# A planned two-stage attention and MoE kernel: the planner's transfer rate, the first w_in pair ahead of k, and new urgencies

## The chip, the cores and the metric

One core of a Trainium2 chip runs the whole kernel. The metric is device time in microseconds (us) of one execution, given as the median of several runs. Engines are named PE (TensorE, matrix products), DVE (VectorE), ACT (ScalarE), POOL (GpSimd) and SP (SyncE, which here only issues DMAs).

## The reference

For 8 batches and 8 heads (576 positions, head size 64), 32 pack queries p attend to k and v, and the packed result then serves as keys and values for the queries q:

```python
def sm_attn(qq, kk, vv):
    s = scale * np.matmul(qq, kk.transpose(0, 1, 3, 2))
    s = s - np.max(s, axis=-1, keepdims=True)
    a = np.exp(s)
    a = a / (np.sum(a, axis=-1, keepdims=True) + 1e-09)
    return np.matmul(a, vv)
p_packed = sm_attn(p, k, v)
out = sm_attn(q, p_packed, p_packed)
...
h = x @ w_in                                   # x: (4608, 512), the heads side by side
sp = np.maximum(h, 0.0) + np.log1p(np.exp(-np.abs(h)))
g = h * erf(sp)
return (g @ w_out).astype(np.float32)          # w_in: (512, 2048), w_out: (2048, 512)
```

The weights w_in and w_out arrive as 64-bit floats, all else as 32-bit floats.

## The kernel before, in words

The second attention is never multiplied out. For each batch b, the packed values are multiplied into w_in once (`w_prime`, tiles `wph`, `wpl`), and the second softmax's weights (tiles `a2h`, `a2l`) then multiply that product to give h. Every operand of the large products is split into a high and a low part (`h` and `l` in the names), and three of the four products of parts are added, so each large product costs three matmuls.

Work comes in units (b, f), 128 columns of the inner dimension of 2048 each: `h_unit` makes h for one unit (two halves c of 288 positions, six matmuls each), copies it to `hs` (line 618), `gate_group` applies softplus (L582) and erf (L587) to a group of units, because each function needs a table load on ACT, and DVE multiplies and splits (L592 to L596); `o_unit` then adds the unit into the output accumulators. The remaining 64 positions per batch are sent to a scratch tensor `rest` and multiplied two batches at a time (`o_rest`). Batches 0 and 1 are interleaved in halves of 8 units, batches 2 to 7 follow with 16 units each.

The head is `attention(0, ...)`. It loads p, k, v and q, makes the scores `s` on PE, the row maxima `ms` and `m` on DVE, the exps on ACT (L451), turns the result over on PE (`t` to `a1t`, `a1r`), multiplies with v (`p`), scales it (`pk`) and turns it into `pt`. Then come the second scores `s<-q,pt`, and on DVE and ACT the second softmax: transposes (L520), maximum (L532), subtraction (L533), exp (L535), sum (L536), reciprocal and scaling (L539), transposes back to `tb` (L542), and the parts `a2h` (L543, ACT) and `a2l` (L544, DVE). In batch 0 this is done in two halves of the positions. The first h product needs the first half of a2 and `w_prime(0, 0)`.

A 64-bit weight tile becomes a 32-bit one in four instructions (`convert`): a scaled copy on ACT (L296), then three bit operations on DVE (L297, L298, L300). The first block of 512 columns of w_in comes in two pairs of row blocks of 1 MB each (`load_w_in_pair`, L329), the later blocks, pieces 1 to 3, in four tiles of 0.5 MB each (`load_w_in`, L314, tiles `wi`), w_out in 16 tiles of 0.5 MB (`load_w_out`, tiles `wos`, then `woh` and `wol`).

The order is not written by hand. Each operation is added to a `Program` with a key (lower is more urgent) and a duration; `Program.order` simulates the engines greedily, always taking the lowest key that is ready, and the start times that it finds fix each engine's order for good: at run time every engine takes its instructions in that order, and each waits for its inputs. The keys are counted in units of h: unit n has key n, its o products n + "lag", h copies n - "copy", softplus n + lag - act - 2, the gate's DVE work n + lag - dve. The keys of attention come from the lists "steady", "second" (batch 1) and "third" (batch 2). Batch 0 has the keys -40, -39, ... by step. The DMA model is two lines:

```python
state["bus"] = max(state["bus"], now + busy + self.SEND[0]) + op.dur / self.SEND[1]
end = state["bus"] + self.SEND[2] + PLAN["late"]
```

with 0.45 us as busy for an issue by SP or ACT, and op.dur the bytes of the transfer. Before the first h, idle times of PE in the plan are filled with small matmuls on `warm`.

Of the kernel before, what the change touches and what calls it, by code (L numbers as in the profile page):

```python
# [18 lines left out]
F64_SCALE = 2.0 ** -112  # L19

PLAN = {
    "lag": 6.48,
    "act": 3.24,
    "dve": 2.85,
    "copy": 11.87,
    "steady": (-0.3, 0.83, 2.16, -1.73, -0.29, 5.48, 1.14, 5.66, 5.08, 10.47, 11.68, 9.06, 11.68, 12.76),
    "second": (-13.65, -15.48, -10.46, -9.6, 0.34, -0.29, -16.5, -2.04, -5.02, 1.53, 1.53, 2.92, 1.21, 6.31),
    "third": (8.44, 9.98, 10.57, 17.02, 19.97, 18.41, 20.11, 22.11, 18.02, 21.6, 23.41, 29.53, 26.07, 28.85),
    "wp": 1.22,
    "wi": 13.75,  # L30
    "wo": 8.18,
    "conv": 2.44,
    "rest": -5.38,
    "ends": (2, 4, 5, 8, 12, 15, 16, 20),
    "merge": (1, 1),
    "turns": (0, 8, 16),
    "second half": 3.65,
    "wp first": 8.52,
    "late": 1.0,
    "first w": (0.1, 0.2),  # L40
    "also": {'norm': 4.02, 'w_out': 5.13, 'packs': 3.76, 'gate': 2.09, 'turned': 2.44},
    "warm": (1.4, 7.0, 1.0),
    "pad": (1.04, 0.1, 0.1),
    "first conv": (-3.79, 0.42),
}


# [22 lines left out]
class Program:  # L70

    LOAD = 1.283
    SWITCH = (0.09, 0.22)
    SEND = (1.0, 380e3, 0.4)

    def __init__(self, room):
        self.ops, self.room = [], room
# [27 lines left out]
    def order(self):  # L105
# [26 lines left out]
        while events:  # L132
# [15 lines left out]
            for engine, line in ready.items():  # L148
# [39 lines left out]
                if engine in ("SP", "POOL") or op.kind == "dma":  # L188
                    state["bus"] = max(state["bus"], now + busy + self.SEND[0]) + op.dur / self.SEND[1]
                    end = state["bus"] + self.SEND[2] + PLAN["late"]  # L190
                else:
# [23 lines left out]
def tile_pack_attention_moe(ctx: ExitStack, tc: tile.TileContext, qT, kT, v, pT, w_in, w_out, out, rest):  # L215
    nc = tc.nc
    P = 128
    B, _, NC, S = qT.shape
# [29 lines left out]
    def buf(tag, shape, name, dtype=F32):  # L248
        pool, bufs = TAGS[tag]
        return Buf(tag, name, lambda: pools[pool].tile(shape, dtype, name=name, tag=tag, bufs=bufs))  # L250
# [7 lines left out]
    def line(engine, ins):  # L258
        names = {last[x] for x in (engine, *fresh) if x in last}
        for name in names:  # L260
            tc.add_manual_dep(ins.ins, name, mybir.DependencyInfo(
                mybir.DependencyClass.NoSync, mybir.DependencyReason.DATA), reason="order")
        for x in (engine, *fresh):
            last[x] = ins.ins.name
        fresh.clear()
        return ins
# [7 lines left out]
    def dve(key, n, emit, w, r, twice=False, after=()):  # L274
        return prog.add("DVE", key, dve_us(n, twice) * PLAN["pad"][0], 0.14 + PLAN["pad"][1], lambda: line("DVE", emit()), w, r, after=after)
# [5 lines left out]
    def dma(key, size, emit, w, r, engine="SP", after=()):  # L281
        return prog.add(engine, key, 0.45 if engine != "POOL" else 1.0, size, lambda: line(engine, emit()), w, r,
                        kind="dma" if engine == "ACT" else 0, after=after)
# [64 lines left out]
    a2, pt, wp = {}, {}, {}  # L348
# [27 lines left out]
    def attention(b, keys):  # L376

        first, roomy = b == 0, b < 2
# [3 lines left out]
        def load(name, src, tag, key, engines=("SP",)):  # L382
            made = []
            for c in range(NC):
                if tag == "wo":
                    made.append([buf("wo", [P, DM], f"{name}{c}{x}_{b}") for x in "ab"])
                    for x in range(2):
                        dma(key, P * HT * 4, lambda c=c, x=x: nc.sync.dma_start(
                            made[c][x][:, 0:HT], src[b, :, c, x * HT:(x + 1) * HT]), (made[c][x],), ())
                else:  # L390
                    made.append(buf(tag, [P, S], f"{name}{c}_{b}"))
                    if not first or name == "q":
                        dma(key, P * S * 4, lambda c=c: nc.sync.dma_start(made[c][:], src[b, :, c, :]), (made[c],), ())
            if first and name == "k":
                for x in range(2):
                    for c in range(NC):
                        at = slice(x * HT, (x + 1) * HT)
                        e, q = (("SP", nc.sync), ("ACT", nc.scalar))[c % 2]
                        dma(key, P * HT * 4, lambda c=c, at=at, q=q: q.dma_start(made[c][:, at], src[b, :, c, at]),
                            ((made[c], x),), (), e)  # L400
            return made
# [4 lines left out]
        def cut(made, c, x):  # L406
            return made[c][x][:, 0:HT] if isinstance(made[c], list) else made[c][:, x * HT:(x + 1) * HT]

        k = load("k", kT, "wo" if b == 1 else "kvq", keys[0])
        vt = "wo" if b < 2 else "kvq"  # L410
        values = [buf(vt, [P, DM if vt == "wo" else S], f"v{j}_{b}") for j in range(NCH)]
# [4 lines left out]
        if first:  # L416
            for i in range(2):
                load_w_in_pair(keys[1] + PLAN["first w"][i], -40 + 8 + PLAN["first conv"][i], 2 * i)
        q = load("q", qT, "kvq" if b else "t0", keys[2])
        big = lambda name, shape: buf("big", shape, f"{name}{b}")  # L420
        a = big("a1_", [P, 2, S])
# [8 lines left out]
        for x in range(2):  # L430
            banks, w, whole = scores[x]
# [85 lines left out]
        for x in range(2):  # L517
            banks, w, whole = places[x]
# [3 lines left out]
        for part in ((0,), (1,)) if first else ((0, 1),):  # L522
# [19 lines left out]
            turned = dve(ks[2], n, lambda span=span: nc.vector.transpose(span(tb), span(ta)), sp, rd)  # L542
# [139 lines left out]
    ends = {*PLAN["ends"], *range(PLAN["ends"][-1], N - G + 1, G), N - 2, N - 1, N}  # L682
# [27 lines left out]
    made = 1  # L710
# [71 lines left out]
```

## Time and profile before

| | |
|---|---|
| median of 3 runs | 726.67 us (725.94 to 727.18) |
| profiled execution | 724.65 us, span 722.9 us |
| PE busy | 705.6 us, 98% |
| ACT busy | 522.1 us, 72% |
| DVE busy | 414.5 us, 57% |
| DMA | 74.79 MB, mean 103 GB/s |

Busy shares are over the whole span, and a busy PE includes the warm matmuls before the first h product. In rows of the timeline the first number is the start in us, the second the time that the row covers; the text in brackets is the idle time of that engine before the row and what ended it. Rows of a stretch give busy time by engine, then the granted clock of TensorE, the busy share of the DMA engines and what they moved. Rows of waits give the total in us, how many, and the longest.

### The profile page before, as it was taken

What the parts mean: (1) busy time and instruction counts of PE and PEld (TensorE: products, weight loads), DVE (VectorE), ACT (ScalarE), POOL (GpSimd) and SP (SyncE); (2) the same over time, 40 slices, a digit from 0 to 9 for tenths busy, and PEclk for the clock granted to TensorE, in tenths of its full rate; (3) what the DMA queues carried; (4) which work ended last, traced back from release to release, by engine and by line L of the source; (5) the groups of instructions that cost most, each with busy time, mean ns of one, the idle gap of its engine ahead of it and who ended that gap; (6) DMA issues with size and microseconds to landing.
All of it is one profiled execution on the core that took longest, in us unless ns stands there. A gap on an engine that the chain in (4) does not pass through costs nothing.

```text
span 722.9 us, 13198 instructions
## 1 busy us (share of the span) xinstructions
PE 705.6 (98%) x5126; PEld 575.8 (80%) x5126; DVE 414.5 (57%) x672; ACT 522.1 (72%) x869; POOL 8.1 (1%) x14
## 2 busy tenths in 40 slices
PE   6979999999999999999999999999999999999997
PEld 5557887878788888887888878787888878788885
DVE  2899987799652375544753166546754247353520
ACT  3399998989885488774976568775987448677841
POOL 0000000001001000000000000000000000000000
PEclk9799999999999999999999999999999999999999
DMA  8952456663507302053204132043122310021113
GB/s 301 335 192 70 129 167 213 223 209 87 115 16 188 102 14 74 16 180 102 72 16 152 58 95 68 16 155 106 39 72 60 121 30 14 17 73 44 44 44 106
DMA packets 66974, 74.79 MB, mean 103 GB/s; under 512 B 40288, under 2 KB 43360, under 8 KB 66912
## 3 DMA queue, kind: packets, MB, share of 16 engines
q1 hardware_dynamic: 65104, 71.14, 32.2%
q0 software_dynamic: 1152, 2.10, 2.1%
q8 instruction: 40, 0.66, 0.4%
q10 hardware_dynamic: 656, 0.72, 0.3%
q14 instruction: 22, 0.18, 0.1%
HBM read 54.00 MB, written 19.92 MB: 102 GB/s over the span
## 4 chain that ended last, share of the span: by engine, by line
PE 86%; ACT 6%; DMA 5%; SPq 1%; issue 0%; DVE 0%; ACTq 0%
PE o L291 47%; PE h L291 26%; PE or L291 6%; PE wp L291 4%; DMA wi<-w_in 2%; PE s L291 2%; DMA q<-qT 1%; PE p L291 1%; ACT L587 1%; DMA v<-v 1%; PE t L471 1%; ACT L582 1%; ACT hs L618 1%; ACT t L582 1%; DMA k<-kT 1%; ACT t L587 1%
## 5 line engine op out<-in xcount | busy, mean ns | idle before, releaser
L291 PE MATMUL o<-woh,gh 128*128 128x512 f32 x512 | 206.4, 403 | 0.0
L291 PE MATMUL o<-woh,gl 128*128 128x512 f32 x512 | 201.9, 394 | 0.0
L291 PE MATMUL o<-wol,gh 128*128 128x512 f32 x512 | 200.8, 392 | 0.0
L618 ACT COPY hs<-h 128x288 f32<-128x288 f32 x256 | 99.3, 393 | 93.7 <-PE h L291 93.0
L291 PE MATMUL h<-a2h,wph 128*128 128x288 f32 x512 | 152.8, 299 | 0.9 <-ACT hs L618 0.8
L291 PE MATMUL h<-a2l,wph 128*128 128x288 f32 x512 | 151.0, 296 | 0.3 <-DVE a2l L544 0.3
L291 PE MATMUL h<-a2h,wpl 128*128 128x288 f32 x512 | 150.4, 294 | 0.0
L592 DVE TENSOR_TENSOR hs<-t,hs 128x576 f32<-128x576 f32 x128 | 94.7, 753 | 78.8 <-ACT t L587 76.9
L291 PEld LDWEIGHTS o<-woh,gh 128*128 128x128 f32 x512 | 96.5, 188 | 33.6 <-issue 18.5
L596 DVE TENSOR_TENSOR gl<-hs,gh 128x576 fp32r<-128x576 f32 x128 | 95.7, 751 | 46.3 <-ACT gh L595 45.7
L291 PEld LDWEIGHTS o<-wol,gh 128*128 128x128 f32 x512 | 96.5, 189 | 22.0
L291 PEld LDWEIGHTS h<-a2h,wph 128*128 128x128 f32 x512 | 96.1, 188 | 13.5 <-ACT hs L618 2.8
L291 PEld LDWEIGHTS o<-woh,gl 128*128 128x128 f32 x512 | 96.7, 189 | 12.4
L291 PEld LDWEIGHTS h<-a2l,wph 128*128 128x128 f32 x512 | 96.1, 188 | 8.6 <-DVE a2l L544 0.5
L291 PEld LDWEIGHTS h<-a2h,wpl 128*128 128x128 f32 x512 | 96.2, 188 | 0.0
L582 ACT ACTIVATE t<-hs 128x576 f32<-128x576 f32 x128 | 87.6, 688 | 2.3
L587 ACT ACTIVATE t<-t 128x576 f32<-128x576 f32 x128 | 84.4, 685 | 0.4
L594 DVE CAST gh<-hs 128x576 fp32r<-128x576 f32 x88 | 39.5, 453 | 37.9 <-PE o L291 37.1
L595 ACT CAST gh<-hs 128x576 fp32r<-128x576 f32 x40 | 27.0, 674 | 30.6 <-PE o L291 22.9
L582 ACT ACT_TABLE_LOAD x37 | 47.5, 1283 | 0.7
L587 ACT ACT_TABLE_LOAD x37 | 47.5, 1283 | 0.7
L291 PE MATMUL or<-woh,g 128*128 128x512 f32 x128 | 39.9, 393 | 0.0
(100 smaller groups left out, 605.1 us busy)
## 6 DMA issues: line engine op xcount, KB each, us to landing
q<-qT SPq DMA_DIRECT2D x32, 288.0 KB, 4.8
v<-v SPq DMA_DIRECT2D x32, 256.0 KB, 3.9
wos<-w_out SPq DMA_DIRECT2D x16, 512.0 KB, 3.6
out<-ob SPq DMA_DIRECT2D x32, 256.0 KB, 2.2
g<-rest SPq DMA_DIRECT2D x16, 512.0 KB, 3.2
k<-kT SPq DMA_DIRECT2D x24, 288.0 KB, 4.2
wi<-w_in SPq DMA_DIRECT2D x12, 512.0 KB, 4.5
rest<-gh SPq DMA_DIRECT2D x128, 32.0 KB, 1.5
```

The source lines that it names most:

```text
L291: return nc.tensor.matmul(*args, **kw)
L471: return [nc.tensor.transpose(tbanks[x]()[:, (j % 2 * 2 + r) * P:(j % 2 * 2 + r + 1) * P], a[:, r, j * P:(j + 1) * P], ident[:]) for j in ...
L582: done.append(act(n + PLAN["lag"] - PLAN["act"] - 2, S, lambda t=t, hs=hs: nc.scalar.activation(t[:], hs[:], AF.Softplus), (t,), (hs,), ru ...
L587: erfs.append(act(e + PLAN["lag"] - PLAN["act"] - 4 + i, S, lambda t=t: nc.scalar.activation(t[:], t[:], AF.Erf), (t,), (), run="erf", kin ...
L592: dve(key, S, lambda t=t, hs=hs: nc.vector.tensor_tensor(hs[:], t[:], hs[:], op=ALU.mult), (hs,), (t,))
L594: op = dve(key, S, lambda hs=hs, ghi=ghi: nc.vector.tensor_copy(ghi[:], hs[:]), (ghi,), (hs,), True)
L595: also("gate", op, "ACT", act_us(S), lambda hs=hs, ghi=ghi: nc.scalar.copy(ghi[:], hs[:]))
L596: dve(key, S, lambda hs=hs, ghi=ghi, glo=glo: nc.vector.tensor_tensor(glo[:], hs[:], ghi[:], op=ALU.subtract), (glo,), (hs, ghi))
L618: op = act(n + c / 2 - PLAN["copy"], HT, lambda c=c, ps=ps: nc.scalar.copy(hs[:, c * HT:(c + 1) * HT], ps[:, 0:HT]), ((hs, c),), (ps,))
```

## The change

The planner's transfer rate goes from 380 to 305 GB/s and the allowance "late" from 1.0 to 0.49 us. The keys of the first two w_in pairs ("first w") go from -38.9 and -38.8 (behind v, whose key is -39) to -42.26 and -39.96: the first ahead of p and k (-40), the second between k and v. Their conversions ("first conv") go from -35.79 and -31.58 to -41.39 and -30.49. Batch 0's k is loaded in four DMAs of whole rows of 576 numbers, two by SP and two by ACT, in place of eight of half rows. All other numbers of PLAN that set urgencies are new; the groups of gated units end at one unit more ("ends").

```diff
-    "lag": 6.48,
-    "act": 3.24,
-    "dve": 2.85,
-    "copy": 11.87,
-    "steady": (-0.3, 0.83, 2.16, -1.73, -0.29, 5.48, 1.14, 5.66, 5.08, 10.47, 11.68, 9.06, 11.68, 12.76),
-    "second": (-13.65, -15.48, -10.46, -9.6, 0.34, -0.29, -16.5, -2.04, -5.02, 1.53, 1.53, 2.92, 1.21, 6.31),
-    "third": (8.44, 9.98, 10.57, 17.02, 19.97, 18.41, 20.11, 22.11, 18.02, 21.6, 23.41, 29.53, 26.07, 28.85),
-    "wp": 1.22,
-    "wi": 13.75,
-    "wo": 8.18,
-    "conv": 2.44,
-    "rest": -5.38,
-    "ends": (2, 4, 5, 8, 12, 15, 16, 20),
+    "lag": 6.45,
+    "act": -6.22,
+    "dve": 0.95,
+    "copy": 7.9,
+    "steady": (-13.39, -9.52, -7.48, -12.06, -11.19, -5.84, -4.63, 4.25, -6.4, 0.25, -3.26, 8.54, -0.72, 10.67),
+    "second": (-17.12, -16.42, -10.18, -8.58, -1.61, -5.6, -21.87, -7.32, -8.94, 1.35, -3.0, 0.16, -0.6, -11.7),
+    "third": (9.42, 9.7, 10.47, 14.11, 16.76, 15.05, 18.66, 20.98, 20.85, 22.32, 25.18, 34.83, 26.33, 31.3),
+    "wp": 1.16,
+    "wi": 13.52,
+    "wo": 11.21,
+    "conv": 1.53,
+    "rest": -1.6,
+    "ends": (1, 2, 4, 5, 8, 12, 13, 16, 20),
...
-    "second half": 3.65,
-    "wp first": 8.52,
-    "late": 1.0,
-    "first w": (0.1, 0.2),
-    "also": {'norm': 4.02, 'w_out': 5.13, 'packs': 3.76, 'gate': 2.09, 'turned': 2.44},
+    "second half": 15.5,
+    "wp first": 9.9,
+    "late": 0.49,
+    "first w": (-3.26, -0.96),
+    "also": {'w_out': 10.23, 'turned': 8.26, 'packs': 2.35, 'norm': 0.2},
...
-    "pad": (1.04, 0.1, 0.1),
-    "first conv": (-3.79, 0.42),
+    "pad": (1.044, 0.076, 0.13),
+    "first conv": (-9.39, 1.51),
+    "whole k": 1,
...
-    SEND = (1.0, 380e3, 0.4)
+    SEND = (1.0, 305e3, 0.4)
...
+                        e, q = (("SP", nc.sync), ("ACT", nc.scalar))[c % 2]
+                        if PLAN["whole k"]:
+                            if x == 0:
+                                dma(key, P * S * 4, lambda c=c, q=q: q.dma_start(made[c][:], src[b, :, c, :]),
+                                    ((made[c], 0), (made[c], 1)), (), e)
+                            continue
                         at = slice(x * HT, (x + 1) * HT)
-                        e, q = (("SP", nc.sync), ("ACT", nc.scalar))[c % 2]
```

"also" names operations that the planner may give to either of two engines, with the key that the other engine adds; the entry "gate" (the copy `gh`, L594 on DVE or L595 on ACT) is gone, so that copy is always on DVE after the change.

## The prediction

> **What bounds the kernel now.** I read the page first, then the table of stretches, then the timeline of the head with what each wait ended on, then the landings of single transfers.
>
> ```profile
> span 722.9 us, 13198 instructions
> ...
> PE 705.6 (98%) x5126; PEld 575.8 (80%) x5126; DVE 414.5 (57%) x672; ACT 522.1 (72%) x869; POOL 8.1 (1%) x14
> ```
> ```profile
> core 0: us, PE busy (x) PEld busy (x) DVE busy (x) ACT busy (x) POOL busy (x), PEclk, DMA share, GB/s
> 10.00:20.00 10.00, 6.08 (x107) 4.72 (x105) 5.29 (x10) 4.73 (x13) 0.00 (x0) 0.77 1.02 378
> 20.00:30.00 10.00, 8.76 (x93) 3.76 (x94) 9.50 (x17) 1.81 (x3) 0.00 (x0) 0.71 1.02 301
> 30.00:40.00 10.00, 9.14 (x74) 8.11 (x72) 7.73 (x19) 6.59 (x16) 0.00 (x0) 1.00 1.02 383
> 40.00:50.00 10.00, 9.04 (x154) 7.06 (x154) 9.79 (x23) 9.94 (x19) 0.00 (x0) 1.00 0.28 83
> 75.00:150.00 75.00, 74.92 (x552) 62.10 (x553) 64.25 (x113) 69.62 (x122) 0.00 (x0) 1.00 0.60 186
> 150.00:700.00 550.00, 550.00 (x3870) 453.84 (x3869) 289.88 (x448) 398.90 (x657) 7.36 (x8) 1.00 0.28 77
> ```
>
> The 98% of PE is an average. From 75 to 700 us PE lacks 0.08 us, and its matmuls are the same ones after the change, so almost nothing can be won there. Before 40 us the sixteen DMA engines are full (share 1.02), VectorE is loaded from 20 us on, ScalarE hardly (1.81 of 10 us). What the change can move is how early PE gets its stream of h products and how full it is up to 75 us. The head, in order of time:
>
> ```profile
> 16.71 1.51 PE L291 MATMUL p<-v,a1t 128*32 128x64 f32 x48 [3.47 <-ACT a1r L486]
> 20.27 2.27 PE L291 MATMUL s<-q,pt 64*32 64x288 f32 x32 [0.36 <-ACT pt L507]
> 22.01 1.18 DVE L300 SCALAR_TENSOR_TENSOR w_in_sb<-w_in_sb 128x1024 uint32<-128x1024 uint32 x1
> 23.11 0.84 DVE L520 STREAM_TRANSPOSE ta<-s 128x288 f32<-128x288 f32 x2
> 25.54 0.74 DVE L532 TENSOR_REDUCE mx<-ta 128x18 f32<-128x576 f32 x1
> 28.21 0.75 DVE L533 TENSOR_TENSOR ta<-ta,mx 128x576 f32<-128x576 f32 x1
> 31.46 0.75 DVE L536 TENSOR_REDUCE mx<-ta 128x18 f32<-128x576 f32 x1 [0.92 <-ACT ta L535]
> 32.13 0.77 DVE L542 STREAM_TRANSPOSE tb<-ta 128x576 f32<-128x576 f32 x1
> 34.54 0.68 ACT L296 ACTIVATE w_in_sb<-wi 128x512 f32<-128x512 f32 x1 [1.00 <-DMA wi<-w_in]
> 35.12 0.66 ACT L543 CAST a2h<-tb 128x576 fp32r<-128x576 f32 x1
> 35.84 0.53 PE L291 MATMUL h<-a2h,wph 128*128 128x288 f32 x2
> 37.22 0.42 DVE L297 TENSOR_SCALAR w_in_sb<-w_in_sb 128x512 uint32<-128x512 uint32 x1
> 40.27 0.51 PE L291 MATMUL h<-a2h,wph 128*128 128x288 f32 x2
> 44.11 0.68 DVE L300 SCALAR_TENSOR_TENSOR w_in_sb<-wi,w_in_sb 128x512 uint32<-128x512 uint32 x1
> 52.14 1.16 PE L291 MATMUL wp<-w_in_sb,pt 64*32 64x512 f32 x16 [2.25 <-DVE ta L520]
> ```
> ```profile
> ACT w_in_sb L296 <- DMA wi<-w_in: 4.9, 3, 3.2
> ACT w_in_sb L296 <- DMA w_in_sb<-w_in: 3.9, 2, 3.1
> ```
>
> The last two rows are the key. ScalarE (ACT) stands 8.8 us in front of conversions of w_in whose data is not there, while work behind them in its fixed order is ready: the a1r copy, for which PE idles 3.47 us; the second exp, for which VectorE (DVE) idles 0.92 us; and the a2h copy, whose input is ready at 32.13 + 0.77 = 32.90 and which starts at 35.12. That is an order made on a belief about transfers. The landings against the belief:
>
> ```profile
> L329 SPq DMA_DIRECT2D w_in_sb<-w_in x1: 576/576/576, 7.7 to 7.7; - x1
> DMA to landing us min/median/max: 7.0/7.0/7.0
> ...
> L393 SPq DMA_DIRECT2D q<-qT x1: 524/524/524, 11.4 to 11.4; - x1
> DMA to landing us min/median/max: 8.9/8.9/8.9
> ```
> ```profile
> 28.01 6.45 DMA wi<-w_in
> ```
>
> Measured: first w_in pair 14.7 us, last chunk of q 20.3, last block of w_in piece 1 34.5. The planner books 0.45 for the issue, 1.0 for the start, all earlier bytes at SEND[1], then 0.4 + "late". The bytes ahead are 3.47, 5.70 and 10.22 MB. At 380 GB/s and late 1.0: 12.0, 17.9, 29.8, so 2.7, 2.4 and 4.7 us too soon. At 305 and late 0.49: 13.7, 21.0, 35.9, that is 1.0 too soon, 0.7 and 1.4 too late. The new belief is nearer at all three points.
>
> The page "DMA: Bandwidth & Descriptors" of the Trainium skill, section Specifications, puts a core's share of HBM at about 358 GB/s; by that, w_in piece 1 would be in at some 31 us, nearer the old belief, and 305 would be a step the wrong way. The trace disagrees: 10.22 MB had arrived at 34.5.
>
> **The change part by part.**
>
> (1) Order of the first transfers. Keys put w_in pair 0 (1.05 MB) at -42.3, p and k at -40, pair 1 at -40 + 0.04, v at -39, q at -38. So pair 0 passes p and k in SP's queue, pair 1 passes the five v issues, and q keeps the same bytes ahead of it. The batch-0 scores then wait for pair 0 as well. Batch 0's k shrinks from eight issues (four SP, four ACT) to four. Rates:
>
> ```profile
> 6.00:8.00 2.00, 1.70 (x24) 0.44 (x16) 0.82 (x2) 0.00 (x0) 0.00 (x0) 1.00 0.86 243
> 14.00:16.00 2.00, 0.00 (x0) 0.00 (x0) 0.04 (x1) 1.19 (x2) 0.00 (x0) 0.87 1.03 407
> 24.00:26.00 2.00, 2.00 (x21) 0.82 (x6) 2.00 (x4) 0.64 (x1) 0.00 (x0) 0.57 0.94 267
> ```
>
> The rows with half-row k (batch 0 before 8 us, batch 1 at 24) move 243 to 267 GB/s, the row with v and w_in 407. If whole rows run at 350, k's 1.18 MB saves up to 1.2 us of transfer; if the size is not the reason, 0. I take 0.5. The same page (Specifications) asks only 512 B of a piece for full rate, and half rows have 1152 B; by it this term is 0 and the sum 0.5 us smaller.
>
> The price: pair 0, p and k are 2.29 MB; at 350 to 267 GB/s from 2 us on they are in at 8.5 to 10.6, and PE now starts its last block of batch-0 scores at 7.60:
>
> ```profile
> 7.60 0.68 PE L291 MATMUL s<-k,p 64*32 64x288 f32 x4 [0.30 <-DMA k<-kT]
> 19.95 0.27 ACT L507 COPY pt<-p 128x128 f32<-128x128 f32 x1 [1.35 <-PE p L504]
> ```
>
> So the scores come 1 to 3 us later. The path from there to pt takes 20.2 - 7.6 = 12.6 us now, of which 3.47 is the wait for a1r and goes, since the conversion of pair 0 then comes before the scores' exps. New pt: 8.5 to 10.6 + 9.2 = 17.7 to 19.8. v, which pt also needs, passes from ahead of both pairs to behind them: its 4.52 MB are in at about 17, and some 2 us of products and small steps follow, 19. q lands at about 19.8. All are at or below q, so the delay of k costs 0, and s<-q,pt starts 0.5 earlier. If that cover is gone, each later us of k is a us of the head.
>
> (2) Conversion of the two pairs. Each takes VectorE 0.69 + 1.23 + 1.2 us. Now the second one's tail (1.18 at 22.01) stands between the first and second transposes of s, which is the path: the second starts at 23.11 in place of 22.01. With pair 0 in at 6 us and pair 1 at about 12, both fit into VectorE's idle half before 20 us. Gain on the path 1.1.
>
> (3) "second half" 3.65 to 15.5 and "conv", "wi" with the new belief. The rows at 25.54, 28.21 and 31.46 are columns of the second half lying in the first half's chain: 0.7 + 0.7 + 0.7 and the 0.92 idle, 3.0; these go behind it. The a2h copy no longer waits for w_in (2.2). First h: 0.5 + 1.1 + 3.0 + 2.2 = 6.8 earlier, about 29.0 in place of 35.84. The second half loses its own waits and, of what stood before it, the pair's tail and the batch-1 maxima and w_in pieces, about 6 too: its h at 40.27 goes to 34.
>
> (4) What is late next. PE has four units of h, then needs w_in piece 1 on VectorE (12 instructions, 4 x (0.42 + 0.68 + 0.68) = 7.1 us, now 37.22 to 44.8), the batch-1 softmax and the first w_out blocks. Its data still lands at 34, at most 1 us earlier, so this stage starts only some 3 to 4 us earlier. Also "ends" has one more gate group: two more table loads.
>
> ```profile
> L582 ACT ACT_TABLE_LOAD x37 | 47.5, 1283 | 0.7
> ```
>
> That is 2.57 us on a ScalarE that is 9.9 of 10 us busy from 40 to 50; off the path it is 0, on it 2.57; I take 1.0, because the smaller first group also lets the first o products come sooner. For the data of piece 1 I take 1.6 (ends 0 and 3.8, the latter if nothing starts earlier than 3 us). Given back: 2.6. The 2.25 us stall at 52.14 (the m bank held by batch 1's second scores until VectorE turns them) I leave in; k of batch 1 now passes v, which may shrink it.
>
> (5) "act", "dve", "copy", "lag", "steady", "third": gates about nine units later against h, attention about ten units earlier. In the steady stage they change the order on ScalarE (73% busy) and VectorE (53%), with PE at 550.00 of 550: cost 0, hidden by PE itself. If that cover goes, 1% of PE idle is 5.5 us. With "gate" out of "also", the gh copies that ACT made go to DVE:
>
> ```profile
> L594 DVE CAST gh<-hs 128x576 fp32r<-128x576 f32 x88 | 39.5, 453 | 37.9 <-PE o L291 37.1
> L595 ACT CAST gh<-hs 128x576 fp32r<-128x576 f32 x40 | 27.0, 674 | 30.6 <-PE o L291 22.9
> ```
>
> 40 x 0.453 = 18.1 us more on DVE, 27.0 us less on ACT over the whole run, under the same cover.
>
> (6) "rest" -5.38 to -1.6 moves the products of the remainders later at the end. The last twelve already run last and end PE:
>
> ```profile
> 715.23 2.73 PE or L291 x12
> ```
>
> The end after it (about 5 us to the span's 722.9) stays; 0, with a bound of +1.5 either way, about half of those products. SP's writes of the remainders and POOL's accumulating stores change only their turn.
>
> **Sum.** -6.8 + 2.6 = -4.2 us. The profiled execution took 724.65 us, 2.0 under the median of 726.67; it would take 720.4, and the median 722.5.
>
> **Rivals.** (A) The earlier h is hidden: PE meets the same wait for w_in piece 1 and w_out at the same time, since their bytes land no sooner. For it: DMA share 1.02 until 40 us. Against it: the 7.1 us of VectorE for piece 1 begin at 37.22, 2.7 after the landing. Given back 6 of 6.8: 726.
>
> (B) Slower, by one mechanism: softplus and erf are put behind the h copies and attention so far that o products lack their gates when the heavy attention of a batch falls into the steady stage. Six batches, from one PE wait of more than 0.7 us in each it beats the gain; at 1 us each, 722.5 + 6 = 728.5. For it: the 9 units of shift. Against: ScalarE is free a quarter of that stage.
>
> (C) The belief of 305 is worse than 380 where few transfers are under way (after 40 us, 83 GB/s), so work stands later than its data allows, and the head gains only its transfer order: (1) and (2), 1.6 us: 725.1.
>
> (D) Everything moves: no give-back, the 2.25 us stall gone: 726.7 - 9.0 = 717.7.
>
> **How the numbers follow.** My forecast has 0.57 (gain 2.5 to 6.5, 720.2 to 724.2), A 0.14, B 0.13, C 0.08, D 0.08. A change under 0.2%, 1.45 us, can't be told from none here. Faster: 0.57 + 0.08 + 0.06 of C + 0.03 of A, 0.74. Same: 0.10 of A, 0.02 of C: 0.12. Slower: B and 0.01 of A, 0.14. The range for 8 in 10 leaves out half of D and most of B: 718.3 to 727.3.
>
> **What would show it.** ScalarE's waits for w_in, 8.8 us now, fall under 3; PE's 3.47 us before p is gone; first h between 28 and 31 us; the next PE wait stands before wp of piece 1 or the first o; 75 to 700 us stays full. I am wrong if s<-q,pt starts after 21 us (k in the way), if first h is early and the start of full PE is not (A), or if PE loses over 1 us between 150 and 700 (B).

## The result, and the profile after

The changed kernel takes 721.73 us (median of 4, 721.21 to 722.06) against 726.31 for the kernel before (4 runs): a ratio of 0.9935 with a 95% interval of 0.9918 to 0.9953, 4.6 us less. The forecast was 722.5. Its size came out by luck: the gain at the head was forecast at 6.8 us and what is given back behind it at 2.6, and both were far off, in opposite directions.

The profiled execution took 722.06 us with a span of 720.3, so span against span the gain is 2.6 us. A further profile of the kernel before, taken for the experiments, had a span of 724.1 (725.92 us), and against that one it is 3.8. The rest of the 4.6 lies in which executions were profiled: those of the kernel before took 1.7 and 0.4 us less than its median, that of the changed kernel 0.3 more than its own.

The page after:

```profile
span 720.3 us, 13230 instructions
...
PE 705.3 (98%) x5159; PEld 576.7 (80%) x5159; DVE 432.6 (60%) x707; ACT 495.8 (69%) x831; POOL 7.9 (1%) x14
...
L588 ACT ACT_TABLE_LOAD x38 | 48.8, 1283 | 0.7
```

PE's sum is the same to 0.3 us. ACT has 26 us less work and DVE 18 more, which is mainly the gh copies going over. One table load more of each kind stands for the extra gate group. By stretches, after:

```profile
10.00:20.00 10.00, 7.72 (x137) 5.78 (x125) 7.28 (x16) 4.39 (x12) 0.00 (x0) 1.00 1.05 348
20.00:30.00 10.00, 9.51 (x134) 7.61 (x135) 8.43 (x19) 2.58 (x4) 0.00 (x0) 1.00 0.87 246
40.00:50.00 10.00, 8.18 (x144) 5.86 (x143) 9.92 (x21) 9.90 (x17) 0.00 (x0) 1.00 0.36 117
36.00:75.00 39.00, 35.83 (x323) 25.66 (x322) 38.24 (x67) 38.72 (x65) 0.00 (x0) 0.96 0.43 143
150.00:700.00 550.00, 550.00 (x3857) 453.93 (x3856) 305.38 (x475) 371.37 (x619) 7.20 (x8) 1.00 0.26 73
```

and the stretch of the kernel before that has no row above:

```profile
36.00:75.00 39.00, 33.92 (x317) 25.60 (x316) 37.93 (x70) 37.44 (x63) 0.00 (x0) 0.96 0.41 131
```

From 150 to 700 us PE is full in both, as forecast. From 36 to 75 us PE is busy 1.9 us more. DVE does 2 us more from 10 to 20 us (7.28 against 5.29). Most of that is batch 0's row maxima (1.54 us at 11.53), which before ran ahead of 10 us; the conversions of the pairs add 0.9. The head after, in order of time:

```profile
7.22 1.14 ACT L297 ACTIVATE w_in_sb<-w_in_sb 128x1024 f32<-128x1024 f32 x1 [5.21 <-DMA w_in_sb<-w_in]
8.78 1.83 PE L292 MATMUL s<-k,p 64*32 64x288 f32 x32 [0.80 <-DMA k<-kT]
9.44 0.64 PEld L292 LDWEIGHTS s<-k,p 64*32 64x32 f32 x24 [0.50 <-DMA k<-kT]
10.39 1.22 DVE L301 SCALAR_TENSOR_TENSOR w_in_sb<-w_in_sb 128x1024 uint32<-128x1024 uint32 x1
11.53 1.54 DVE L440 TENSOR_REDUCE ms<-s 128x1 f32<-128x288 f32 x4
15.49 1.14 ACT L297 ACTIVATE w_in_sb<-w_in_sb 128x1024 f32<-128x1024 f32 x1
16.51 1.08 ACT L485 COPY a1t<-t 128x512 f32<-128x512 f32 x2
20.82 1.21 PE L292 MATMUL s<-q,pt 64*32 64x288 f32 x32 [0.35 <-ACT pt L513]
21.65 1.67 DVE L526 STREAM_TRANSPOSE ta<-s 128x288 f32<-128x288 f32 x4 [1.57 <-PE s L292]
23.24 1.37 DVE L538 TENSOR_REDUCE mx<-ta 128x18 f32<-128x576 f32 x2
25.66 1.42 DVE L539 TENSOR_TENSOR ta<-ta,mx 128x576 f32<-128x576 f32 x2
27.36 1.40 DVE L542 TENSOR_REDUCE mx<-ta 128x18 f32<-128x576 f32 x2
30.52 0.72 DVE L548 STREAM_TRANSPOSE tb<-ta 128x576 f32<-128x576 f32 x1
31.37 0.69 ACT L297 ACTIVATE w_in_sb<-wi 128x512 f32<-128x512 f32 x1 [3.57 <-DMA wi<-w_in]
32.68 0.66 ACT L297 ACTIVATE w_in_sb<-wi 128x512 f32<-128x512 f32 x1 [0.62 <-DMA wi<-w_in]
33.24 0.66 ACT L549 CAST a2h<-tb 128x576 fp32r<-128x576 f32 x1
33.95 0.53 PE L292 MATMUL h<-a2h,wph 128*128 128x288 f32 x2 [1.64 <-ACT a2h L549]
35.98 0.50 ACT L457 ACTIVATE a<-s,m 128x288 f32<-128x288 f32 x1
48.47 0.50 PE L292 MATMUL o<-woh,gh 128*128 128x512 f32 x1 [0.46 <-DVE gh L600]
```

The second scores start later than before (20.82 against 20.27), first h earlier by 1.9 (33.95 against 35.84), and the first o product stands at 48.47, in the place where PE used to wait 2.25 us ahead of `wp`. Before, the first o came after that wait.

The start of batch 1's exps (L457) turns out to be a mark that the end follows. In the kernel before it is the second of these rows. The first is the first maximum of the second softmax, which the row at 23.24 above shows for the changed kernel:

```profile
23.88 0.71 DVE L532 TENSOR_REDUCE mx<-ta 128x18 f32<-128x576 f32 x1
37.88 0.49 ACT L451 ACTIVATE a<-s,m 128x288 f32<-128x288 f32 x1
```

In the changed kernel the exps are 1.9 us earlier, too. From there ACT hardly rests: it is busy 38.72 of the 39 us from 36 to 75 after, 37.44 before (the rows of that stretch above).

### The profile page after: what moved, and what is told of

Same layout as the page of the kernel before. It is cut to its first block, busy times and chain, and to the rows that moved or that the text cites. A ratio compares the mean times of both kernels' runs of the same rounds, so it can differ in the third digit from the quotient of the medians.

```text
span 720.3 us, 13230 instructions
## 1 busy us (share of the span) xinstructions
PE 705.3 (98%) x5159; PEld 576.7 (80%) x5159; DVE 432.6 (60%) x707; ACT 495.8 (69%) x831; POOL 7.9 (1%) x14
## 3 DMA queue, kind: packets, MB, share of 16 engines
q0 software_dynamic: 1152, 2.10, 2.2%
## 4 chain that ended last, share of the span: by engine, by line
PE 83%; ACT 11%; DMA 3%; SPq 1%; issue 1%; DVE 0%; ACTq 0%
PE o L292 45%; PE h L292 25%; PE or L292 6%; PE wp L292 4%; PE s L292 2%; ACT L593 1%; ACT t L593 1%; ACT L588 1%; ACT hs L624 1%; ACT t L588 1%; DMA v<-v 1%; PE p L292 1%; DMA q<-qT 1%; DMA wi<-w_in 1%; PE t L477 1%; ACT w_in_sb L297 1%
## 5 line engine op out<-in xcount | busy, mean ns | idle before, releaser
L600 DVE CAST gh<-hs 128x576 fp32r<-128x576 f32 x128 | 58.0, 456 | 77.6 <-PE o L292 76.1
L654 ACT COPY ob<-o 128x512 f32<-128x512 f32 x40 | 22.8, 587 | 24.8 <-PE o L292 24.7
```

Source lines behind the costliest of these rows:

```text
L600: op = dve(key, S, lambda hs=hs, ghi=ghi: nc.vector.tensor_copy(ghi[:], hs[:]), (ghi,), (hs,), True)
L654: act(key - 1, DM, lambda: nc.scalar.copy(ob[:], to[:]), (ob,), (to,))
```

## The experiments

Theories: **belief** (the truer transfer rate gives an order with fewer waits), **order** (the first w_in pair ahead of k and whole rows of k), **urgencies** (the new keys together). Later two more about what sets the end: **first h** and **ACT stage** (the end is a fixed distance behind the start of batch 1's exps).

**e1, the rate alone.** In the kernel before:

```diff
-    "late": 1.0,
+    "late": 0.49,
-    SEND = (1.0, 380e3, 0.4)
+    SEND = (1.0, 305e3, 0.4)
```

> The kernel before with the planner's rate at 305 GB/s and late at 0.49, nothing else changed. Theory belief (the gain comes from an order that fits the landings): the a1t copy goes ahead of the first w_in conversion, PE's 3.5 us wait before p shrinks below 1, first h at 33 to 35 us, 723 to 725 us. Theory order (the gain comes from sending the first pair ahead of k): 726 to 727, no change. Theory urgencies (the new keys are what counts): 725.5 to 728.

Measured: 729.85 us, ratio 1.0046 (1.0031 to 1.0061), slower. First h did come earlier, at 34.42, but PE lost more behind it:

```profile
PE h L291 <- ACT hs L618: 3.1, 5, 0.9
PE h L291 <- ACT wph L565: 1.7, 1, 1.7
PE p L291 <- ACT a1r L486: 1.4, 1, 1.4
PE wp L291 <- DVE ta L520: 1.2, 1, 1.2
```

The rate alone brings first h forward by 1.4 us and loses more behind it. A redrawn order can cost as much by itself (e7), so this says only that the rate alone doesn't give the gain.

**e2, the transfer order alone.** In the kernel before (the code for whole rows of k, as in the change, is left out here):

```diff
-    "first w": (0.1, 0.2),
+    "first w": (-3.26, -0.96),
-    "first conv": (-3.79, 0.42),
+    "first conv": (-9.39, 1.51),
+    "whole k": 1,
...
```

> The kernel before with the first w_in pair ahead of k, the conversions' keys of the change and k in whole rows; rate 380 and all other keys as before. Theory order: first conversion done by 12 us, first h 1 to 2 us earlier, 723 to 725. Theory belief: ACT still stands before w_in data, k comes 1 to 3 us later, 726 to 729. Theory urgencies: 725.5 to 728.

Measured: 732.03 us, ratio 1.0076 (1.0063 to 1.0089). First h is at 36.88 and the exps of batch 1 only at 41.15. Theory order falls as a gain that stands by itself.

**e3, the change without its transfer order.**

```diff
-    "first w": (-3.26, -0.96),
+    "first w": (0.1, 0.2),
-    "first conv": (-9.39, 1.51),
+    "first conv": (-3.79, 0.42),
```

> The changed kernel with the two w_in pairs again behind v and their conversions' old keys; rate 305, whole rows of k and all other keys stay. Theory belief: keeps most of the gain, 721.5 to 723.5, first h within 1 us of 33.95. Theory order: loses it, 725 to 727, first h at 35 to 36. Theory urgencies: 721.5 to 723.5 as well.

Measured: 720.53 us, ratio 0.9921 (0.9910 to 0.9933). The whole gain stays, and the median is 1.2 us better than the change's, by intervals that overlap. Its rows on ACT and PE:

```profile
32.09 0.65 ACT L549 CAST a2h<-tb 128x576 fp32r<-128x576 f32 x1
34.84 0.49 ACT L457 ACTIVATE a<-s,m 128x288 f32<-128x288 f32 x1
...
32.80 0.53 PE L292 MATMUL h<-a2h,wph 128*128 128x288 f32 x2 [0.56 <-ACT a2h L549]
33.59 0.53 PE L292 MATMUL h<-a2l,wph 128*128 128x288 f32 x2 [0.26 <-DVE a2l L550]
```

First h and the exps are both 1.1 us earlier than in the change, and the end is 1.3 earlier (span 719.0 against 720.3). Behind the head the instructions stand in nearly the same order as in the change (see the table below), so this is close to a test of the named part alone: the first pair ahead of k carries none of the gain.

**e4, k in half rows again.** `"whole k": 1` to `0` in the changed kernel.

> The changed kernel with k of batch 0 again in eight half-row transfers. If whole rows save transfer time (0.5 us in the prediction, 0 to 1.2 the bounds): the scores' last block starts 0.5 to 1.2 us later than 8.8 us, and the time is 0 to 1 us more, 721.7 to 722.7. If halves help because the first half's scores start sooner: scores start earlier and the time is the same or 0.5 less.

Measured: 724.68 us, ratio 0.9977 (0.9967 to 0.9987), 3 us more than the change and outside what I expected. The stall is back:

```profile
51.14 1.96 PE L292 MATMUL wp<-w_in_sb,pt 64*32 64x512 f32 x16 [2.34 <-DVE ta L526]
53.03 0.79 PE L292 MATMUL o<-woh,gh 128*128 128x512 f32 x1
```

The first o is behind `wp` again. The planner drew another order here, so e5 parts what the transfers do from what the planner makes of them.

**e5, half rows with the order kept.** The planner sees whole rows; each transfer is sent as two:

```diff
-    dma(key, P * S * 4, lambda c=c, q=q: q.dma_start(made[c][:], src[b, :, c, :]),
+    dma(key, P * S * 4, lambda c=c, q=q, e=e: (line(e, q.dma_start(made[c][:, 0:HT], src[b, :, c, 0:HT])),
+                                    q.dma_start(made[c][:, HT:S], src[b, :, c, HT:S]))[1],
```

> The changed kernel with the planner's order kept to the letter, each whole-row transfer of batch 0's k sent as two half-row transfers. This parts what the transfers do from what the planner makes of them. If half rows themselves cost what undoing them cost (3 us): 724 to 725. If it was the reshuffled order: first scores 0.5 to 1.2 us later than 8.78, 721.5 to 722.8.

Measured: 722.41 us, ratio 0.9949 (0.9936 to 0.9961). Half rows themselves cost about 0.7 us, by intervals that overlap, so that 0 is not excluded; the other 2.3 of e4 are the planner's reshuffled order.

**e6, the first a2h ahead of the conversions.** Two of ACT's places changed in the planned order:

```diff
...
+    for op in convs:
+        if his[0].start - 8 < op.start < his[0].start and op is not convs[0] and op is not convs[1]:
+            op.start = his[0].start + 0.001
...
```

> The changed kernel with one edit to ACT's order: the first a2h copy goes ahead of the two conversions of w_in piece 1 that it stands behind. First h at 32.0 in place of 33.95. If the time goes with first h: 1.5 to 2 us less, 719.7 to 720.5. If a later wait (second half of a2, wp of piece 1) takes it: 721 to 722.

Measured: 721.86 us, ratio 0.9941 (0.9927 to 0.9955): no gain. First h was at 33.83, not 32.0, since the second scores started at 21.46 and ran at half clock (2.17 us in place of 1.21). The 1.64 us before first h were gone, so the edit did its part, and the exps of batch 1 began at 35.97, as in the change. What the edit is worth at an equal clock, this profile doesn't show.

**e7, a setting that means nothing.** In the changed kernel, the planner's factor on ACT's and DVE's durations:

```diff
-    "pad": (1.044, 0.076, 0.13),
+    "pad": (1.046, 0.076, 0.13),
```

> The changed kernel with a setting that means nothing for the design moved by 0.2%: the planner's factor on the durations of ACT and DVE 1.046 in place of 1.044. If the keys as such carry the gain, the time stays within 0.7 us of 721.7. If the gain is that of one lucky order among many near ones, it moves by 1 to 6 us, most likely up.

Measured: 725.04 us, ratio 0.9984 (0.9972 to 0.9996). 3.3 of the 4.6 us go. And the head is better than the change's: the exps start 1.3 us sooner. The loss is behind it:

```profile
34.70 0.49 ACT L457 ACTIVATE a<-s,m 128x288 f32<-128x288 f32 x1
...
49.80 1.96 PE L292 MATMUL wp<-w_in_sb,pt 64*32 64x512 f32 x16 [2.34 <-DVE ta L526]
51.70 0.80 PE L292 MATMUL o<-woh,gh 128*128 128x512 f32 x1
```

**e8, the kernel before once more,** for a second profile.

> The kernel before once more, for a second profile: its runs spread over 3 us, from 724.7 to 727.7, and the profiled one was at the fast end. If the spread sits in the head, first h moves by 1 to 2 us against 35.84; if later, the waits of PE between 36 and 75 us differ from 5.1 us or the granted clock does.

Measured: 725.92 us (one run), span 724.1. First h is at 36.53 (0.7 later than in the first profile), the exps at 38.57 (0.7 later), and PE's waits from 30 to 160 us add up to 6.6 in place of 5.1. The spread between executions sits in both places.

**The sum of it.** The span, less the start of batch 1's exps, in us:

| kernel | exps of batch 1 | span | rest |
|---|---|---|---|
| before; e8; e12 | 37.88; 38.57; 37.93 | 722.9; 724.1; 723.2 | 685.0; 685.5; 685.3 |
| after | 35.98 | 720.3 | 684.3 |
| e3 | 34.84 | 719.0 | 684.2 |
| e5 | 37.02 | 721.0 | 684.0 |
| e6 | 35.97 | 720.1 | 684.1 |
| e9 | 33.10 | 717.3 | 684.2 |
| e10 | 34.75 | 719.2 | 684.5 |
| e4; e7 | 36.05; 34.70 | 723.4; 723.5 | 687.4; 688.8 |
| e2; e1; e11 | 41.15; 37.38; 35.23 | 729.5; 728.5; 726.3 | 688.4; 691.1; 691.1 |

Six kernels with nearly the change's order behind the head have a rest of 684.0 to 684.5, though their heads differ by 3.9 us. (In their traces 96% or more of ACT's instructions from 36 to 150 us stand in the change's order; in e4, e7 and e11 55 to 65% do.) The kernel before has 685.0 to 685.5, the reshuffled orders 687.4 to 691.1. So the time is a head, up to the exps, and a rest that goes with the order. e9 to e12 were chosen when this table had only the rows up to e8.

**e9, e3 with the first a2h ahead** (the edit of e6 in e3).

> The changed kernel with the old place of the w_in pairs, and the first a2h copy ahead of the conversions of w_in piece 1 on ACT. Theory first h (the time follows the first h product): first h 1 us earlier than 32.80, 719.5. Theory ACT stage (the time is the start of batch 1's exps, where ACT's full stage begins, plus 684.2 us): VectorE loses its 0.64 us wait before a2l, so the exps start at 34.2 in place of 34.84, 719.9; the difference to no gain is within the noise here.

Measured: 719.65 us, ratio 0.9911 (0.9898 to 0.9925), the fastest kernel here; the profiled execution took 719.05.

```profile
30.10 0.67 ACT L550 CAST a2h<-tb 128x576 fp32r<-128x576 f32 x1 [3.48 <-DVE tb L549]
33.10 0.50 ACT L458 ACTIVATE a<-s,m 128x288 f32<-128x288 f32 x1
```

The exps start 1.7 us sooner than in e3 and the span is 1.7 shorter. This profile's second scores were also early (18.35 against 19.68), so not all of the 1.7 is the edit; the medians differ by 0.9 and their intervals overlap.

**e10, the exps earlier at the cost of h's second product.** In e9, DVE's second transpose and batch 1's maxima go ahead of the first a2l:

```diff
...
+    if tbs[1].start > los[0].start:
+        los[0].start = tbs[1].start + 0.001
+    after_tb = tbs[1].start
+    for i, op in enumerate(m_ops):
+        assert op.start > after_tb
+        op.start = after_tb + 0.0002 * (i + 1)
...
```

> As the run with the old place of the pairs and a2h first, and on VectorE the second half's last transpose and batch 1's maxima go ahead of the first half's a2l, which frees the exps' buffer and input sooner and makes the first h's second product later by 0.8 us. Theory ACT stage: exps of batch 1 start at 33 to 33.5, time 718.3 to 719. Theory first h: 720 to 721, since h gets its a2l later.

Measured: 720.00 us, ratio 0.9914 (0.9901 to 0.9928), no better than e9. The exps came at 34.75, not 33 to 33.5, because ACT had the conversion of another block of w_in in front of the second a2h, whose data landed late in this execution, the slowest of the five (721.00 us). The profile is still of use:

```profile
31.99 0.51 PE L292 MATMUL h<-a2h,wph 128*128 128x288 f32 x2
33.66 0.53 PE L292 MATMUL h<-a2l,wph 128*128 128x288 f32 x2 [1.16 <-DVE a2l L554]
```

First h is 0.8 us earlier than in e3, the exps 0.1 earlier, the span 0.2 longer. So the end did not go with the first h product. It may go with the exps or with h's second product, which needs a2l and moved by only 0.1 (33.66 against 33.59 in e3): in the six kernels the span less the start of that second product is 684.9 to 685.6, nearly as steady as the table's rest, and less the first product 685.3 to 687.2. No run parts the first two, and this is one pair of profiles.

**e11, the old gate keys, and the old list "also" with them.** In the changed kernel:

```diff
-    "act": -6.22,
-    "dve": 0.95,
-    "copy": 7.9,
+    "act": 3.24,
+    "dve": 2.85,
+    "copy": 11.87,
...
-    "also": {'w_out': 10.23, 'turned': 8.26, 'packs': 2.35, 'norm': 0.2},
+    "also": {'norm': 4.02, 'w_out': 5.13, 'packs': 3.76, 'gate': 2.09, 'turned': 2.44},
```

> The changed kernel with act, dve, copy and also as before: softplus and erf urgent again, gh copies shared with ACT. Rate, transfer order and all other keys stay. If the gates' lateness is what lets ACT serve attention first, the gain falls by 2 to 4 us (724 to 726). If steady-stage keys are free, 721.5 to 722.5. If any reshuffle costs, 724 to 728, with the stall before wp of piece 1 (2.3 us) back.

Measured: 728.08 us, ratio 1.0035 (1.0021 to 1.0048), 6.4 us more than the change, from a head that is 0.75 us earlier:

```profile
36.00:75.00 39.00, 32.29 (x306) 23.82 (x307) 37.50 (x65) 38.68 (x63) 0.00 (x0) 0.96 0.37 119
...
PE h L292 <- ACT hs L624: 3.5, 5, 1.2
PE h L292 <- ACT wph L571: 1.4, 1, 1.4
```

PE waits for copies of h on ACT, and is 3.5 us less busy from 36 to 75 than in the change. The loss is larger than the 3.3 us that the meaningless edit of e7 made. Late gates, or the shorter list "also" that came with them, may thus be a real part of the gain, but one redrawn order can't be told from them.

**e12, the same kind of edit in the kernel before.** `"pad": (1.04, ...)` to `(1.042, ...)`.

> The kernel before with the planner's duration factor 1.042 in place of 1.04. If the kernel before was itself one good order among near ones: slower by 1 to 6 us, 727 to 732. If its order is ordinary: within 1.5 us of 726.3, either sign.

Measured: 725.46 us, ratio 0.9994 (0.9985 to 1.0004), no change. The order of PE, DVE and ACT up to 150 us stayed nearly as it was, with the stall at `wp`. So this edit hardly redrew the order, and doesn't show what a redraw would have cost this kernel.

## Why the prediction was right, and which steps failed

**What bounds the kernel.** Right: PE is at 550.00 of 550 from 150 to 700 us after as before, and all that was won lies ahead of 75 us.

**Step (1), the transfers' order: wrong sign.** The forecast was 0.5 us earlier second scores; they came 0.55 later, and taking the order back (e3) made the kernel 1.2 us faster, by intervals that overlap. The bytes came within my bounds: with whole rows they moved at 400 to 419 GB/s,

```profile
4.00:6.00 2.00, 2.00 (x13) 2.00 (x12) 0.00 (x0) 0.00 (x0) 0.00 (x0) 1.00 1.03 419
6.00:8.00 2.00, 1.98 (x19) 1.74 (x16) 0.00 (x0) 0.78 (x1) 0.00 (x0) 1.00 1.05 400
8.00:10.00 2.00, 1.22 (x28) 0.55 (x32) 1.57 (x2) 0.36 (x1) 0.00 (x0) 1.00 1.05 413
```

and the last of k was in at about 9.4 (PE's row at 9.44), in the middle of my 8.5 to 10.6. What failed is the 9.2 us from there to `pt`: up to the second scores 11.4 us passed. The conversions do come before the exps, but they are not free. Pair 0 landed at 7.2, not 6, since ACT sends its half of k beside it from 0.77 us on. Its last DVE instruction (10.39 to 11.61) stood in front of the maxima, and the second pair's on ACT (15.49) in front of the a1t copies. The wait that I took away was replaced by two of about 1 us.

Whole rows were worth about 0.7 us (e5), with 0 not excluded, which is within my bounds; but the reading behind that term was wrong. In the stretch at 243 GB/s that I took for half rows of k, 71% of the bytes were v's, in rows of 2048 B. From 4 to 6 us before, 71% were half rows of k, and in e4 from 6 to 8 us 97% (shares by the packets of the traces):

```profile
4.00:6.00 2.00, 1.65 (x14) 0.36 (x16) 0.00 (x0) 0.00 (x0) 0.00 (x0) 1.00 1.02 347
```
```profile
6.00:8.00 2.00, 0.10 (x1) 0.02 (x1) 0.00 (x0) 0.49 (x1) 0.00 (x0) 1.00 1.08 371
```

So stretches of mostly half rows reached 347 and 371 GB/s. The row at 267 from 24 to 26 was half rows alone, as I read it.

The page "DMA: Bandwidth & Descriptors" of the Trainium skill, section Specifications, gives about 358 GB/s as the limit of one core, half of what an HBM stack moves. The rows at 400 to 419, with one core at work, are over it, and the measurement decides.

**Step (2), the pairs' conversions off the path: 1.1 us forecast, 1.2 measured, with luck.** The four transposes run in one piece now (21.65 to 23.32, before 21.60 to 24.98), and from the start of the second scores to the first maximum it takes 2.4 us (20.82 to 23.24) in place of 3.6 (20.27 to 23.88). Part of that is the clock, which I had not priced at all:

```profile
18.00:20.00 2.00, 1.67 (x27) 0.77 (x18) 1.98 (x3) 0.65 (x2) 0.00 (x0) 0.50 1.04 386
```

is before, with a granted clock of 0.50; after and e6, which have the same work on PE in that stretch:

```profile
18.00:20.00 2.00, 1.24 (x64) 0.98 (x64) 1.97 (x3) 0.02 (x1) 0.00 (x0) 1.00 1.08 324
```
```profile
18.00:20.00 2.00, 1.94 (x64) 1.68 (x64) 1.82 (x2) 0.00 (x1) 0.00 (x0) 0.50 1.09 327
```

At 0.50 the 32 second scores take 2.17 (e6) to 2.27 us (before), at 1.00 1.21 (after). All three profiles of the old order (before, e8, e12) have 0.50 there, and of the change's order e5 and e6 have 0.50 as well; whether the order has a part in it isn't shown. The page "TensorE: Matmul & The Clock Gate" of the Trainium skill, Part 1, says that the window that decides is free-running and the switch varies from run to run; e6 against after agrees.

**Step (3), first h: 1.9 us in place of 6.8.** Besides step (1), two terms failed. "Second half" did not put the second half behind the first: the pairs at 25.66 and 27.36 are both halves', since a greedy planner takes what is ready whatever its key. From the first maximum to the first half's `tb` it takes 8.0 us (23.24 to 31.24) in place of 9.0 (23.88 to 32.90), so 1.0 of the 3.0 us came. And the a2h copy still stands behind conversions of w_in: `tb` is ready at 31.24, the conversions start at 31.37 and 32.68, the copy at 33.24. That is 2.0 us of delay in place of 2.2, so 0.2 of the 2.2 came. The four parts, -0.55, 1.2, 1.0 and 0.2, make the 1.9. ACT's waits for w_in did not fall under 3 but are 9.4 in all; the 5.21 at 7.22 are harmless, with nothing ready behind them. The truer rate did not remove the delay, because the planner had `tb` too late: in its plan the copy starts at 33.25, as soon as `tb` is there, 2.0 us after the real `tb`. First h, at 33.95, missed the 28 to 31 that I had named as a sign.

**Step (4), what is given back: -0.7 us in place of +2.6.** The 6.8 had been earned on paper only, so there was little to give back. The stall before `wp`, which I left in, went: six o products of the first gate group, now a single unit, run there. That is a turn of the order, not a property of the group: e4 and e7 have the same groups and the stall.

**Step (5), urgencies at 0: the wrong place.** The steady stage is indeed covered in the change. But from 36 to 75 us, where ACT is full, the order decides: there e11, with the gates' keys and "also" as before, has PE 3.5 us less busy (and 1.2 less from 150 to 700, so the cover is not complete for every order). Rival B did not come: late gates did no harm (550.00 of 550), and e11 points the other way.

**Step (6), the end: as forecast.** From the end of PE's last product to the end of the span it takes 4.9 us after (715.39 to 720.3) and 5.0 before (717.95 to 722.9).

So 4.2 was reached by 6.8 - 2.6, where the traces have 1.9 + 0.7 (2.6 in the profiled pair, 3.8 with the second profile of before) and the medians 4.6. The direction and range were right; the account was not, and that the median came within 0.8 us is luck. What carries the gain is the new keys together with the new rate, since e3 keeps it without the transfer order. Which of them does, and how much of it is one lucky order among near ones, is open: the rate alone costs 3.8 us (e1), and neither the keys with the old rate nor more redraws were tried.

## What to carry to other kernels

Where a greedy planner fixes the order, one number changed anywhere can draw a new order, and here a meaningless 0.2% was worth 3.3 us in one kernel (e7), while in another it hardly changed the order (e12): undo a part with the order held (e5 against e4) before naming it as the cause, and run a meaningless edit to know how much a reshuffle alone is worth. Look for the mark that the end follows at a fixed distance: here it was the start of ACT's full stage, or h's second product beside it, and not the first product on PE. A transfer sent earlier brings its conversion earlier too, and that can then stand in front of other work on engines with a fixed order (10.39 and 15.49 in the head).

## What the runs showed of the hardware that was not expected

The same PE order ran at a granted clock of 0.50 or 1.00 from 18 to 20 us in different executions (e6 and after), worth 1 us on 32 score products. Loads with rows of 2304 B and 4096 B moved at 400 to 419 GB/s. Rows of 1152 B moved at 371 in e4 from 6 to 8 us, and at 267 in the kernel before from 24 to 26, so their length alone doesn't set the rate; with the order held, half rows of batch 0's k cost the kernel about 0.7 us, with 0 not excluded.
